# Sketched attention and a squared-ReLU FFN on one core: order of loads, casts, squares and GpSimd work

## The chip, the core and the metric

The kernel runs on one core of a Trainium2 chip. The core has a matrix engine (TensorE, PE in the profile), three engines for elementwise work (VectorE or DVE, ScalarE or ACT, GpSimd or POOL), and DMA engines that move data between memory (HBM) and the on-chip memories. A DMA is issued from an engine's instruction stream: here from SyncE (SP), which does nothing else, and from ScalarE. Each engine works through its own instructions in the order in which the program gives them, and waits where an instruction needs something that another engine has not yet finished. The metric is the device time of one execution in microseconds (us), told as the median of several runs.

## The reference

The input is q, k and v for 4 batches, 4 heads, 1088 tokens and 32 columns a head, two small sketches S1 and S2 (8 x 32), and two weights w_in (128 x 2048) and w_out (2048 x 128). All are 32-bit floats.

```
phi(x) = outer product of (S1 x) and (S2 x), 64 features a token
kv  = sum over tokens of phi(k) v          (64 x 32 a head)
z   = sum over tokens of phi(k)            (64 a head)
x   = phi(q) kv / (phi(q) z + 1e-6)        (heads side by side: 128 columns)
out = relu(x w_in)^2 w_out                 (4 * 1088 = 4352 tokens)
```

## The kernel before

The FFN is nearly all of the matrix work. Each batch of 1088 tokens is cut into column chunks of 384, 384 and 320 tokens, and the 2048 hidden features into 16 blocks of 128. One FFN step is one chunk with one block: 4 x 3 x 16 = 192 steps. In a step, `ffn1` (L677) multiplies the block of w_in, which is held as 16-bit floats, with the chunk of x into the PSUM tile `pg` (two buffers), a relu goes from `pg` to the SBUF tile `gt` (three buffers; on ScalarE at L691 or on VectorE at L693), and a square goes from `gt` to `g2` (on ScalarE at L697, or on VectorE or GpSimd at L699). `ffn2` (L703) multiplies the block of w_out with `g2`, in 32-bit floats, and adds it up in the PSUM tile `po` over the 16 blocks. `ffn2` of a step stands three steps behind `ffn1` of the same step in TensorE's order (LA = 3). So TensorE's order is: ffn1 of step i + 3, ffn2 of step i, then whatever attention work is placed in slot i. When a chunk is finished, VectorE scales and transposes `po` (`f_oT` and `f_ob` L767 for the first two chunks, `f_sc` and `f_sT` after), and SP writes it out.

The attention of the first chunk has to come before the first FFN step and forms the prologue (L826 to L926). In short: `s_nat` (L143) receives S1 and S2, is transposed into `s_T`, and is spread into several small layouts; k is transposed on VectorE (`a_kT`), multiplied with the sketch (`a_kf`), and its features are formed (`a_fs`, `a_kp`); `a_kv` (L306) and `a_z` add up kv and z; `a_kvz` transposes them (`kvt`) and spreads them (`kvz`); q is transposed (`a_qT`), multiplied with the sketch (`rep`, L847) and its products are formed; `a_nd` gives numerator and denominator; `a_x1`, `a_x2` (L604) and `a_x3` (L628) on VectorE divide, and scale each row by a factor so that it fits 16-bit floats (the output is multiplied by the factor's square, `beta`, later; `f_br` L735 spreads beta to 16 x 3 columns with 16 small GpSimd copies); `a_xp` and `a_xT` turn x. `keep_warm` (L826) gives TensorE matmuls on zeros while it has nothing else to do.

The loads of batch 0 (L143 to L177) stand in this order: ScalarE issues S1, S2 and later the last part of v; SP issues k in two pieces, q columns 0 to 383, v in eight pieces, q columns 384 to 1087, w_in in two halves, w_out in two halves. Eight completion semaphores are shared in turn by all these DMAs, so a DMA's issue also waits for the landing of the one eight before it. w_in is cast to 16 bits by two ScalarE copies of 1024 columns (L903).

The attention of all other chunks is put into the FFN steps. A small planner, `_Plan` (L24), keeps for each engine the time that is already placed in each step. `add` puts a task into the first step that is at least a fixed lag behind the tasks it needs and in which the engine's placed time with this task stays under a limit (0.95 us for TensorE, 1.2 and later 0.99 for VectorE, 0.6 for ScalarE, 5.0 for GpSimd). Tasks are added in the order in which they need each other: `old_chunk` (the second chunk of batch 0, in the prologue's style), then per chunk `feature_tasks` (the q products: `a_qg` on TensorE, shuffles `sh` on VectorE, multiplies `qpn` on GpSimd), `nd_tasks` (`a_ndn`), `x_tasks` (the division: `dT`, `de`, `rd`, `rb`, `x` on VectorE, `ax` on ScalarE, `sm` on TensorE, `rs` and `s` (`a_s2`) on VectorE, `xs` and `bt` on GpSimd; `xs` writes the tile `xT` that ffn1 of the next chunk reads), and per batch `k_tasks` and `kv_tasks` (`kp` half on VectorE, half on GpSimd; the sums `ks` on GpSimd; `a_kv9` on TensorE). Several of them use the same two PSUM buffers in turn (the planner's keys "N" and "X"): `a_kv9` of batch 1 can start only when `s` of the last chunk of batch 0 has read its buffer.

After that, `balance` (L1067) goes through the steps in order and chooses for each one which engine does its relu and which its square, by the estimated lateness of each engine. Then the main loop writes the program: for each step ffn1 with its relu and square, ffn2, and the tasks of that slot, in this order on every engine:

```
for i in range(NS + 4):
    if i + LA < NS:
        ffn1(i + LA, where[i + LA])
    if 0 < i < NS - NFF:
        ffn2(i)
    ...
    for f, args in P.slots[i]:
        f(*args)
```

The last chunk is handled apart: its steps form the output of one tile with tokens as rows, so that the end is short (`ffn2_tile`).

## Time and profile before

| what | value |
|---|---|
| time, median of 11 runs | 196.01 us (195.56 to 198.5) |
| the profiled execution's own time | 195.47 us |
| its span, first to last instruction | 193.6 us |
| mean TensorE clock granted | 0.996 of full |
| ffn2 matmuls (L709) | 143.8 us busy, mean 458 ns |
| ffn1 matmuls (L681) | 61.1 us busy, mean 317 ns |
| relu on ScalarE (L691) / VectorE (L693) | 124 of 457 ns / 69 of 533 ns |
| square on ScalarE (L697) / GpSimd (L699) | 159 of 506 ns / 31 of 774 ns |
| HBM traffic | 8.78 MB read, 2.23 MB written |

The profile comes from one execution. In its lines a place in the code is given as L and the line number of the listing above; an operation is written as output, arrow, input, with tile names. Busy times of TensorE add up to more than its share since matmuls overlap in the engine's pipeline: what counts there is the distance between the starts of successive matmuls. The timeline lists instructions as start, duration, engine, line, operation, shape and count (x2 means two alike were merged into one line); a bracket at the end tells how long the engine stood idle before and what released it. The chain of waits follows the end of the program back, at each instruction, to what released it. The table of stretches gives for each stretch of time its length, then busy time and instruction count for TensorE, its weight loads, VectorE, ScalarE and GpSimd, then the clock, the share of time at which the DMA engines were busy, and GB/s.

### The profile page before, as it was taken

To read this page: it belongs to the slowest core of one execution; us is meant where nothing else is said; L and a number is where in the kernel's file an instruction comes from. 1 tells how busy PE (TensorE), PEld (TensorE's weight loads), DVE (VectorE), ACT (ScalarE), POOL (GpSimd) and SP (SyncE) were. 2 spreads that over 40 slices of the span, in tenths; PEclk is the share of its full clock that TensorE was granted. 3 is DMA by queue.
4 is the path that set the end of the run, shared out by engine and by line. 5 is a ranking of instruction groups with operands and counts; after the bars stand their busy time and mean duration, and the time that the engine had idled before them with its cause. 6 is when DMAs were issued, how large, how long until landed. Compare 5 with 4: busy or idle time off the path is not lost.

```text
span 193.6 us, 4446 instructions
## 1 busy us (share of the span) xinstructions
PE 185.4 (96%) x1639; PEld 112.5 (58%) x1639; DVE 131.5 (68%) x326; ACT 141.2 (73%) x322; POOL 97.5 (50%) x162
## 2 busy tenths in 40 slices
PE   7997999989999999999999999999999999999990
PEld 2873755555666555565566555565566555556990
DVE  2966886985787559954876659864776555667740
ACT  3454996976787969866897969867787868767740
POOL 3844546990393838941473557951483932600000
PEclk9999999999999999999999999999999999999998
DMA  6799410020037320020057410020020110110201
GB/s 188 201 317 280 117 51 2 3 41 3 0 59 207 124 34 3 2 44 0 2 98 182 123 22 3 5 39 0 0 44 2 19 20 0 20 20 0 41 3 34
DMA packets 27199, 11.40 MB, mean 59 GB/s; under 512 B 19178, under 2 KB 25770, under 8 KB 27178
## 3 DMA queue, kind: packets, MB, share of 16 engines
q1 hardware_dynamic: 26726, 11.02, 23.2%
q8 instruction: 13, 0.21, 0.5%
q10 hardware_dynamic: 452, 0.10, 0.2%
q14 instruction: 8, 0.07, 0.1%
HBM read 8.78 MB, written 2.23 MB: 57 GB/s over the span
## 4 chain that ended last, share of the span: by engine, by line
PE 86%; DVE 7%; DMA 1%; ACT 1%; issue 1%; POOL 0%; ACTq 0%; DVEq 0%; POOLq 0%
PE po L709 54%; PE pg L681 15%; PE ndn L448 4%; PE kvp L314 3%; PE pt L726 2%; DMA s_nat<-in_S_dram 1%; PE qg L417 1%; PE rep L847 1%; PE kf L258 1%; DVE sh L426 1%; PE kvp L328 1%; PE kf L357 1%; PE kvp L576 1%; DVE ob L770 1%; PE sm L498 1%; PE nd L576 1%
## 5 line engine op out<-in xcount | busy, mean ns | idle before, releaser
L709 PE MATMUL po<-g,w_o 128*128 128x384 f32 (+3 forms) x386 | 143.8, 458 | 0.0
L697 ACT ACTIVATE g<-gt 128x384 f32<-128x384 f32 (+1 forms) x159 | 79.9, 506 | 21.3 <-DVE gt L693 17.6
L709 PEld LDWEIGHTS po<-g,w_o 128*128 128x128 f32 x386 | 66.1, 190 | 32.6 <-issue 22.5
L691 ACT ACTIVATE gt<-pg 128x384 f32<-128x384 f32 (+2 forms) x124 | 56.2, 457 | 13.8 <-PE pg L681 13.0
L681 PE MATMUL pg<-xT,w_in 128*128 128x384 f16 (+2 forms) x193 | 61.1, 317 | 0.7 <-ACT xT L660 0.3
L693 DVE TENSOR_SCALAR gt<-pg 128x384 f32<-128x384 f32 (+1 forms) x69 | 36.7, 533 | 26.5 <-PE pg L681 25.4
L699 POOL TENSOR_TENSOR g<-gt 128x384 f32<-128x384 f32 (+1 forms) x31 | 23.8, 774 | 47.1 <-ACT gt L691 46.8
L681 PEld LDWEIGHTS <-w_in 128*128 128x128 f16 x193 | 18.8, 98 | 24.0 <-issue 6.6
L435 POOL TENSOR_TENSOR qp<-sh 128x384 f32<-128x384 f32 (+1 forms) x20 | 19.1, 961 | 6.9 <-DVE sh L426 5.1
L426 DVE STREAM_SHUFFLE sh<-qg 128x384 f32<-128x384 f32 (+1 forms) x40 | 21.4, 562 | 0.0
L458 DVE STREAM_TRANSPOSE dT<-ndn 128x384 f32<-128x384 f32 (+1 forms) x10 | 5.4, 543 | 11.3 <-PE ndn L448 11.3
L284 POOL TENSOR_TENSOR kp<-fs 128x1152 f32<-128x1152 f32 x3 | 9.5, 3167 | 5.3 <-DVE fs L277 5.3
L522 POOL TENSOR_TENSOR xT<-x,rs 128x384 f16<-128x384 f32 (+1 forms) x10 | 9.5, 947 | 1.7 <-DVE rs L513 1.7
L741 POOL COPY br<-beta 32x3 f32<-32x3 f32 x32 | 6.5, 204 | 5.6 <-DVE beta L642 4.3
L448 PE MATMUL ndn<-qp,kw 64*32 64x192 f32 (+1 forms) x320 | 8.4, 318 | 0.0
L531 POOL TENSOR_TENSOR bt<-s 128x384 f32<-128x384 f32 (+1 forms) x10 | 7.8, 781 | 0.9 <-DVE s L504 0.9
L448 PEld LDWEIGHTS ndn<-qp,kw 64*32 64x32 f32 x320 | 4.7, 106 | 5.2 <-issue 3.8
L340 POOL TENSOR_TENSOR ks<-kp 128x1024 f32<-128x1024 f32 x3 | 7.1, 2366 | 0.2
L513 DVE TENSOR_SCALAR rs<-sm 128x384 uint32<-128x384 uint32 (+1 forms) x10 | 5.2, 522 | 2.5 <-PE sm L498 2.5
L314 PE MATMUL kvp<-kp,vn 128*32 128x64 f32 (+1 forms) x288 | 5.9, 221 | 0.7 <-DVE s L504 0.7
L351 POOL TENSOR_TENSOR ks<-ks 128x512 f32<-128x512 f32 (+1 forms) x6 | 6.2, 1032 | 0.5
L314 PEld LDWEIGHTS kvp<-kp,vn 128*32 128x32 f32 (+1 forms) x288 | 4.7, 109 | 2.8 <-DVE s L504 1.3
(119 smaller groups left out, 157.3 us busy)
## 6 DMA issues: line engine op xcount, KB each, us to landing
vn<-in_v_dram SPq DMA_DIRECT2D x32, 64.0 KB, 4.0
kn<-in_k_dram SPq DMA_DIRECT2D x3, 544.0 KB, 11.2
qn<-in_q_dram SPq DMA_DIRECT2D x3, 544.0 KB, 3.6
out_dram<-oT SPq DMA_DIRECT2D x24, 48.0 KB, 1.9
w_in<-in_moe_w_in_dram SPq DMA_DIRECT2D x2, 512.0 KB, 4.7
w_o<-in_moe_w_out_dram SPq DMA_DIRECT2D x2, 512.0 KB, 9.5
out_dram<-oT SPq DMA_DIRECT2D x12, 40.0 KB, 1.7
out_dram<-ob SPq DMA_DIRECT2D x8, 48.0 KB, 1.8
```

What stands on the lines that cost most here:

```text
L284: (nc.vector if g == 0 else nc.gpsimd).tensor_tensor(out=_ap(st[b, "kp2"], 0, 128, 128 * NT * g, [[64, 2 * NT], [8, 8], [1, 8]]), in0=_ap( ...
L314: nc.tensor.matmul(st[b, "kvp"][32 * h : 32 * h + 32, 0:64], _ap(vn[b], 0, n, v0 + dv * h, [[1, 32]]), kp[0:n, at[h] : at[h] + 64], start= ...
L426: nc.vector.stream_shuffle(in_=_ap(st[b, "qg", ch], 0, 128, 0, [[512, 2], [1, n]]), out=_ap(t_, 0, 128, 0, [[n, 2], [1, n]]), mask=mask_q[ ...
L435: nc.gpsimd.tensor_tensor(out=qp[:, 0 : 2 * n], in0=st[b, "sh", ch, s, 0][:, 0 : 2 * n], in1=st[b, "sh", ch, s, 1][:, 0 : 2 * n], op=mult,)
L448: nc.tensor.matmul(nd[32 * h : 32 * h + 32, 512 * g + 192 * i : 512 * g + 192 * i + n], st[b, "kw"][64 * g : 64 * g + 64, 128 * i + 32 * h ...
L522: nc.gpsimd.tensor_tensor(out=st[b, "xT"][:, 384 * ch : 384 * ch + n], in0=st[b, "x", ch][:, 0:n], in1=st[b, "rs", ch][:, 0:n], op=mult,)
L681: nc.tensor.matmul(pg[:, c0:c1], w_in[:, 128 * c : 128 * c + 128], st[b, "xT"][:, 384 * ch + c0 : 384 * ch + c1],)
L691: nc.scalar.activation(gt[:, c0:c1], pg[:, c0:c1], Relu)
L693: nc.vector.tensor_scalar(out=gt[:, c0:c1], in0=pg[:, c0:c1], scalar1=0.0, scalar2=None, op0=amax)
L697: nc.scalar.activation(g2[:, c0:c1], gt[:, c0:c1], Square)
L699: (nc.vector if on[1] == "DVE" else nc.gpsimd).tensor_tensor(out=g2[:, c0:c1], in0=gt[:, c0:c1], in1=gt[:, c0:c1], op=mult)
L709: nc.tensor.matmul(st["po", b, ch][:, c0:c1], w_o[:, 128 * c : 128 * c + 128], g2s[i][1][:, c0:c1], start=first, stop=(c == NFF - 1), skip ...
```

## The change

Loads: S2 is issued by SP as its second DMA (ScalarE keeps S1); q columns 384 to 1087 are loaded in two pieces; SP's order behind v becomes w_in first half, q 384 to 767, w_out first half, q 768 to 1087, w_in second half, w_out second half. The unused rows of the last tile of v are set to zero, and the kv sum of that tile runs over 128 rows instead of 64.

Prologue: the transpose of q columns 384 to 767 moves from behind the numerators to before `kvt`; that of the other columns moves to the end of the prologue. ScalarE casts only the first half of w_in; the second half becomes two casts of 512 columns on GpSimd, the first two tasks of GpSimd in the FFN steps. `a_qg` for the third chunk moves from the prologue to behind the ffn1 of step 2, and `f_br` of the first chunk into the FFN steps. `a_x2` gets by with four VectorE operations instead of five: the scale is a power of two taken from the float's exponent bits, and beta is formed from the same bits behind `xs` by two operations instead of one.

FFN steps: a square on ScalarE is no longer written directly behind its relu, but kept in a list (`due`) and written behind the relu of the next step; in the last chunk it stays where it was. The planner gives GpSimd tasks intervals of time (length divided by 0.85) instead of a limit per step, with the finish of the interval counted for what follows; some assumed durations change (kp 2.7 to 3.15, ks2 2.0 to 2.3, br 2.4 to 3.6); `balance` takes the length of a step and of its relu and square from the columns, and gives GpSimd no square in a step whose successor has a GpSimd task. The tasks' slots and the engines for relu and square are worked out anew from this.

```
@@ _Plan @@
-        self.late = []
+        self.pool = []
...
+        if eng == "POOL":
+            d, t = dur / 0.85, float(s)
+            for t0, t1 in sorted(self.pool):
+                if t + d <= t0:
+                    break
+                t = max(t, t1)
+            self.pool.append((t, t + d))
+            s = int(t)
+            self.fix(key, eng, dur, s, f, *args)
+            self.at[key] = max(s, int(t + d - 0.6))
+            return s
@@ loads of batch 0 @@
-    def load_qk(dst, src, b, c0, c1):
-        nc.sync.dma_start(
+    def load_qk(dst, src, b, c0, c1, eng=nc.sync):
+        eng.dma_start(
...
-    for s_, r0 in ((S1, 0), (S2, 8)):
-        nc.scalar.dma_start(s_nat[r0 : r0 + 8, :], s_[:, :])
+    nc.scalar.dma_start(s_nat[0:8, :], S1[:, :])
...
-    nc.scalar.copy(zero_a[:, :], zero[:, 0:8])
     alloc_loads(0)
     load_qk(kn[0], k, 0, 0, 512)
+    nc.sync.dma_start(s_nat[8:16, :], S2[:, :])
     load_qk(kn[0], k, 0, 512, S)
     load_qk(qn[0], q, 0, 0, 384)
     load_v(vn[0], 0, 0)
     load_v(vn[0], 0, 2, (nc.scalar, nc.scalar))
+    nc.scalar.copy(zero_a[:, :], zero[:, 0:8])
     load_v(vn[0], 0, 1)
-    load_qk(qn[0], q, 0, 384, S)
     w_in32 = cpool.tile([128, DFF], F32)
     w_in = cpool.tile([128, DFF], F16)
     w_o = cpool.tile([128, DFF], F32)
-    for c in range(2):
-        nc.sync.dma_start(
+    def load_w_in(c, eng):
+        eng.dma_start(
             w_in32[:, 1024 * c : 1024 * c + 1024], moe_w_in[:, 1024 * c : 1024 * c + 1024]
         )
-    for c in range(2):
+    def load_w_o(c):
         nc.sync.dma_start(
             _ap(w_o, 0, 128, 1024 * c, [[128, 8], [1, 128]]),
             bass.AP(
...
             ),
         )
+    def w_cast(c0, n, copy):
+        copy(w_in[:, c0 : c0 + n], w_in32[:, c0 : c0 + n])
+    load_w_in(0, nc.sync)
+    load_qk(qn[0], q, 0, 384, 768)
+    load_w_o(0)
+    load_qk(qn[0], q, 0, 768, S)
+    load_w_in(1, nc.sync)
+    load_w_o(1)
...
+    nc.gpsimd.memset(vn[0][64:128, 1024:1152], 0.0)
@@ a_kv @@
-        n = 64 if b == 0 and t == 8 else 128
+        n = 128
@@ a_x2, a_x3 @@
-        mm, mp, rm = (small(x, 1) for x in ("mm", "mp", "rm"))
-        nc.vector.tensor_tensor(out=m1[:, :], in0=mx[:, :], in1=rden[:, :], op=mult)
+        mm, rm = (small(x, 1) for x in ("mm", "rm"))
+        nc.vector.scalar_tensor_tensor(
+            out=m1[:, :], in0=mx[:, :], scalar=1e-20, in1=rden[:, :], op0=amax, op1=mult
+        )
         nc.vector.tensor_reduce(
             out=mm[:, :], in_=_ap(m1, 0, 128, 0, [[4, 3], [1, 4]]),
             axis=AX, op=amax, apply_absolute_value=True,
         )
         nc.vector.tensor_scalar(
-            out=mp[:, :], in0=mm[:, :], scalar1=1.0 / 1024.0, scalar2=1.0 / 1024.0,
-            op0=mult, op1=add,
-        )
-        nc.vector.reciprocal(rm[:, :], mp[:, :])
-        nc.vector.tensor_tensor(
+            out=rm[:, :].bitcast(U32), in0=mm[:, :].bitcast(U32),
+            scalar1=EXP, scalar2=EXP, op0=band, op1=bxor,
+        )
+        nc.vector.scalar_tensor_tensor(
             out=_ap(sc, 0, 128, 0, [[4, 3], [1, 4]]),
-            in0=_ap(rden, 0, 128, 0, [[4, 3], [1, 4]]),
+            in0=_ap(rden, 0, 128, 0, [[4, 3], [1, 4]]), scalar=512.0,
             in1=_ap(rm, 0, 128, 0, [[1, 3], [0, 4]]),
-            op=mult,
-        )
-        st[b, "x2", ch] = sc, mp
+            op0=mult, op1=mult,
+        )
+        st[b, "x2", ch] = sc, mm
...
         if o + n == 3:
-            nc.vector.tensor_tensor(
-                out=st[b, "beta"][:, 3 * ch : 3 * ch + 3], in0=mp[:, :], in1=mp[:, :], op=mult,
+            mp = wpool.tile([128, 3], F32, tag="mp", name="mp")
+            nc.vector.tensor_scalar(
+                out=mp[:, :].bitcast(U32), in0=mm[:, :].bitcast(U32),
+                scalar1=EXP, scalar2=None, op0=band,
+            )
+            nc.vector.scalar_tensor_tensor(
+                out=st[b, "beta"][:, 3 * ch : 3 * ch + 3], in0=mp[:, :], scalar=2.0**-20,
+                in1=mp[:, :], op0=mult, op1=mult,
             )
@@ ffn1 @@
+    due = []
+    def square_due():
+        while due:
+            dst, src = due.pop()
+            nc.scalar.activation(dst, src, Square)
...
+        square_due()
         if on[1] == "ACT":
-            nc.scalar.activation(g2[:, c0:c1], gt[:, c0:c1], Square)
+            due.append((g2[:, c0:c1], gt[:, c0:c1]))
+            if i >= NS - NFF:
+                square_due()
         else:
             (nc.vector if on[1] == "DVE" else nc.gpsimd).tensor_tensor(
@@ prologue @@
         a_z(0, *st[0, "kp", t], t == 8)
     nc.scalar.copy(qb[:, 0:128], rep[2, 0][:, 0:128])
     products(0, 128)
+    a_qT(0, 384, 768)
...
     a_kvs(0)
-    for c in range(2):
-        nc.scalar.copy(
-            w_in[:, 1024 * c : 1024 * c + 1024], w_in32[:, 1024 * c : 1024 * c + 1024]
-        )
+    w_cast(0, 1024, nc.scalar.copy)
     for t in range(3):
         a_nd(0, t)
-    a_qT(0, 384, S)
     a_qc(0, 1, psf, "po")
-    a_qg(0, 2)
...
     a_qb(0, 1)
-
-
-    f_br(0, 0)
+    a_qT(0, 768, S)
     P = _Plan(NS + 4, {"PE": 0.95, "DVE": 1.2, "ACT": 0.6, "POOL": 5.0, "SP": 9.0})
@@ tasks, planner, balance @@
-        P.add(("br", b, ch), "POOL", 2.4, [("x3", b, ch)], f_br, b, ch)
...
-            P.add(("kp", n, g), ("DVE", "POOL")[g], (1.36, 2.7)[g], [("fs", n, g)], a_kp2, n, g)
+            P.add(("kp", n, g), ("DVE", "POOL")[g], (1.36, 3.15)[g], [("fs", n, g)], a_kp2, n, g)
...
-        P.add(("ks2", n), "POOL", 2.0, [("ks1", n)], a_ks2, n)
+        P.add(("ks2", n), "POOL", 2.3, [("ks1", n)], a_ks2, n)
...
+    for i in range(2):
+        P.fix(("w", i), "POOL", 0.65, i, w_cast, 1024 + 512 * i, 512, nc.gpsimd.tensor_copy)
+        P.pool.append((float(i), i + 0.7))
     feature_tasks(0, 2)
+    P.add(("br", 0, 0), "POOL", 3.5, [], f_br, 0, 0)
...
+        if n == 1:
+            P.add(("br", 0, 1), "POOL", 3.6, [("x3", 0, 1)], f_br, 0, 1)
...
-            w = 0.8 if steps[s_][1] < 2 else 0.667
-            cost = {"ACT": 0.48 * w / 0.8, "DVE": 0.56 * w / 0.8, "POOL": 0.95 * w / 0.8}
-            time = w + load["PE"][s_]
+            n1, n2 = (min(384, S - 384 * steps[i_][1]) for i_ in (s_ + LA, s_))
+            cost = {"ACT": (n1 + 30) / 960, "DVE": (n1 + 140) / 960, "POOL": (n1 + 20) / 440}
+            time = n1 / 2400 + n2 / 600 + load["PE"][s_]
...
-                if q_ == "POOL" and (late[q_] + own_[q_] > 1.0 or end_ >= -1):
+                if q_ == "POOL" and (late[q_] + own_[q_] > 1.0 or load["POOL"][s_ + 1] > 0 or end_ >= -1):
@@ main loop @@
         ffn1(i, ("ACT", ("DVE", "ACT")[i % 2]))
+    a_qg(0, 2)
     for cols in ((0, 128), (128, 384)):
         ffn2(0, cols)
...
         if i + LA < NS:
             ffn1(i + LA, where[i + LA])
+        else:
+            square_due()
```

More of the change, by code (lines that the diff above doesn't have):

```diff
@@ L633, in a_x3 @@
             st[b, "xs", ch] = wpool.tile([128, 3 * 128], F16, tag="xs", name="xs")
-        sc, mp = st[b, "x2", ch]
+        sc, mm = st[b, "x2", ch]
         nc.vector.tensor_tensor(
@@ L823, in last_tile, with keep_warm @@
         store(b, 6, ob, 128, nc.sync)
-    def keep_warm(n, cols=512):
+    def keep_warm(n):
         t_ = st["warm"]
         for _ in range(n):
-            nc.tensor.matmul(t_[:, 0:cols], zero[:, 0:128], zero[:, 0:cols])
+            nc.tensor.matmul(t_[:, 0:512], zero[:, 0:128], zero[:, :])
     st["warm"] = psf.tile([128, 512], F32, tag="pg", name="warm")
```

## The prediction

> **What bounds the kernel now.** I read the page first: busy time and the chain that ended last.
>
> ```profile
> PE 185.4 (96%) x1639; PEld 112.5 (58%) x1639; DVE 131.5 (68%) x326; ACT 141.2 (73%) x322; POOL 97.5 (50%) x162
> PE 86%; DVE 7%; DMA 1%; ACT 1%; issue 1%; POOL 0%; ACTq 0%; DVEq 0%; POOLq 0%
> ```
>
> TensorE carries 86% of the chain. From 19.65 us on, the timeline of TensorE shows one FFN step each 0.81 us for 384 columns (0.67 for 320), which is the length of its own matmuls. Those are not touched, so a gain can come only from the stretch before the first FFN matmul (16.93 us) and from places where TensorE leaves this spacing. The chain of waits up to 20 us gives the first (start, length, work):
>
> ```profile
> 1.55 2.80 DMA s_nat<-in_S_dram
> ...
> 4.48 0.21 DVE s_T L229
> ...
> 11.00 1.49 PE rep L847 x6
> 12.49 1.51 PE kvp L576 x12
> ...
> 15.38 0.18 DVE mp L615
> 15.59 0.19 DVE rm L619
> ```
>
> S1 and S2 set the first 4.4 us; DVE's small operations carry it from 14.1 to 16.0. The timeline of TensorE gives the second:
>
> ```profile
> 38.63 0.81 PE L709 MATMUL po<-g,w_o 128*128 128x384 f32 x2
> 39.40 0.32 PE L681 MATMUL pg<-xT,w_in 128*128 128x384 f16 x1
> 40.33 0.32 PE L681 MATMUL pg<-xT,w_in 128*128 128x384 f16 x1
> 40.49 0.81 PE L709 MATMUL po<-g,w_o 128*128 128x384 f32 x2
> 42.01 1.21 PE L314 MATMUL kvp<-kp,vn 128*32 128x64 f32 x72 [0.71 <-DVE s L504]
> ```
>
> The ffn1 matmuls stand 0.93 apart instead of 0.81 (two steps, 0.26 lost), and the kv matmuls come at 42.01 where 40.49 + 0.65 + 0.1 = 41.24 was possible (0.77 lost). That is 1.03 us, the only such place before 178 us; near 179 us another 0.3 is lost in the last chunk, whose order the change leaves alone. Why 0.93? ScalarE's timeline:
>
> ```profile
> 33.76 0.47 ACT L691 ACTIVATE gt<-pg 128x384 f32<-128x384 f32 x1
> 34.26 0.53 ACT L697 ACTIVATE g<-gt 128x384 f32<-128x384 f32 x1
> 34.69 0.47 ACT L691 ACTIVATE gt<-pg 128x384 f32<-128x384 f32 x1
> ...
> 64.54 0.85 ACT L691 ACTIVATE gt<-pg 128x384 f32<-128x384 f32 x2
> ```
>
> Relu to its own square takes 0.50 from start to start, square to the next relu 0.43: 0.93 a pair, TensorE's spacing at 39 us. Where two relus follow one another (64.54: two of 0.47 in 0.85) the second starts 0.85 - 0.47 = 0.38 after the first. Waiting for the relu's result thus costs about 0.13 per pair.
>
> **The change part by part, on the profiled execution** (195.47 us, span 193.6; the median of the runs, 196.01, lies 0.54 above it, and I add the sum to the median).
>
> *S2 on SP's queue, second.* Before, ScalarE issues S1 at 0.93 and S2 at 1.55, which lands some 2.8 us later. On SP it is issued at about 1.2, behind the first k load, which landed at 3.47 (0.75 + 2.7). s_T then waits for DVE's first transpose (3.50 + 0.71 = 4.21) and not for 4.48: -0.3; bounds 0 and -0.34. SP's later DMAs move: from the third v load on, each waits for an older DMA's landing (8.8 us of issue for what takes 0.47 each), so little of S2's 0.47 is left at w_in; I count 0.2.
>
> *q columns 384 to 767 transposed before kvt.* DVE idles 0.99 us there (10.07 to 11.07), and the transpose takes 0.53 (as qT at 5.92), so it is free if the data is there. But this DMA now stands behind 512 KB of w_in.
>
> ```profile
> 6.63 0.43 SPq L110 DMA_DIRECT2D qn<-in_q_dram  x1
> 7.11 0.90 SPq L166 DMA_DIRECT2D w_in<-in_moe_w_in_dram  x2
> ...
> ```
> ```profile
> 7.70:11.00 3.30, 3.30 (x150) 2.78 (x149) 1.95 (x4) 0.55 (x3) 2.92 (x12) 1.00 0.96 266
> 11.00:12.40 1.40, 1.40 (x8) 1.02 (x7) 0.98 (x3) 0.73 (x3) 1.16 (x6) 1.00 1.00 393
> ```
>
> v's packets end at about 7.7; 512 + 192 KB (0.72 MB) at 266 GB/s (last column) take 2.7 us, at 393 GB/s 1.8. With 0.2 for S2 and 0.35 to land (as the difference between packets and landing of the first k load) the q columns arrive between 10.1 and 11.0. DVE is ready at 9.8, kvz is needed by 11.8 (rep's products start then), so arrival up to 10.45 is free and each later tenth costs a tenth: 0 to +0.8, I take +0.3, near the slower window, which has the same w_in half in it. Queued behind the waiting transpose are kvt, kvz and the products, and for them the nd matmuls.
>
> *x2 in four operations instead of five.* One of 0.2 from start to start falls out of the chain (15.38 to 15.59): -0.2. The extra operation for beta stands behind xs, beside the transposes on TensorE: 0.
>
> *Second half of w_in cast on POOL, 2 x 512 columns.* ScalarE loses a cast of 1.05 that ended at 14.2, idle until 16.6: 0. POOL's price: its CAST of 128 columns takes 0.29; its MEMSETs of 128 and 384 columns (0.21, 0.42) rise 0.85 ns a column, its multiplies 1.7, so 0.6 to 0.9 each. They are needed at FFN step 8, after 23 us; that cover is 6 us. What they can hurt is DVE. The lines:
>
> ```profile
> 32.39 3.12 POOL L284 TENSOR_TENSOR kp<-fs 128x1152 f32<-128x1152 f32 x1 [1.22 <-DVE fs L277]
> ...
> 34.40 1.14 DVE L467 TENSOR_SCALAR de<-dT 128x10 f32<-128x10 f32 x1
> ```
>
> A TENSOR_SCALAR on ten columns (0.17 elsewhere) lasted until POOL's multiply ended at 35.51. w_in's second half is now behind 0.36 MB of q, 0.5 MB of w_in and 0.5 MB of w_o, the same bytes that ended before at about 14.0; landed at 14.2 to 14.8, the casts run somewhere in 14.2 to 16.3, over x2 (14.98 to 16.0). Bounds: 0, and +1.2 if a small operation waits out each cast. Nearest in kind, a copy with one input, are POOL's copies of beta at 19.3 to 20.1: the DVE square beside them took 0.56, its usual time, and it was POOL that waited. So I take +0.2 and keep +1.2 for the range.
>
> [...]
>
> *qg of chunk 2 moved from TensorE's idle time (14.74) to behind ffn1 of step 2.* 16 matmuls, 0.50, and 0.1 for each change between kinds (the steps around ndn show it). In that place TensorE still loses 0.3 to 0.4 to relu (18.17, then 19.17 for 18.97), so of 0.7 I count +0.3; bounds 0 and +0.7. Its q columns arrive before 14, transposed on DVE behind qb (0.47, beside relu).
>
> *Squares a step behind.* A pair costs 0.37 + 0.43 = 0.80 in place of 0.93, TensorE's own 0.81. The 0.26 goes. The 0.77 goes too: kv9 is put five steps later, and the second half of its sum (POOL, 2.27 at 38.03) no longer stands beside ob, which took 1.62 instead of 0.56 there; s is then ready one us sooner. -1.0, bounds -0.3 and -1.1. What is late next: a square now ends about 0.8 later, and ffn2 reads it three steps after ffn1 began. For 384 columns: ready 0.43, relu, square and relu in turn 1.17, square 0.52, sum 2.1 of 2.6. For 320: 0.38 + 1.0 + 0.47 = 1.85 of 2.13, and an ax between (0.5) overruns it by 0.2. Three such chunks, of which the planner gives the first no relief on DVE: +0.2, bounds 0 and +0.9.
>
> *The rest: 0.* br (16 copies, 3.5) moves into POOL's idle time, needed at 34; if POOL were late, ob and its DMAs alone would wait. The interval bookkeeping puts xs as near as four steps (2.7 us) before its chunk; rs 0.55, xs 1.0 and waits make 2.0, so 0.7 of cover. vn's memset runs at 1.4, long before use.
>
> Sum: -0.3 + 0.3 - 0.2 + 0.2 + 0.3 - 1.0 + 0.2 = -0.5: 196.0 - 0.5 = 195.5 us.
>
> **The rivals.** (a) *The casts block x2*: +1.2 instead of +0.2, sum +0.5, 196.5, slower. For: the 1.14 row and the arrival estimate. Against: the copies at 19.3. It decides from a cast cost of 1.1 on. (b) *q waits behind w_in*: +0.8, sum 0, 196.0, no change. For: 0.96 DMA share at 7.7 to 11. Against: 393 GB/s right after. (c) *Squares late*: +0.9, sum +0.2, 196.2. For: 0.28 of slack only; against: DVE and POOL take relus and squares in most such steps. (d) *xs late at a chunk's start*: 0.7 of cover used up, 0.4 at four chunks: +1.1 on the sum, 196.9. For: four steps instead of nine and more; against: POOL is half idle. (e) *The start gains all it can*: q and casts free, qg in the idle 0.3: 194.8.
>
> **How the numbers follow.** 0.2% is 0.39 us, about what a measurement of this kernel can tell from no change. Chances: forecast 0.45 (its own range 194.9 to 195.8; 0.42 faster, 0.03 same), (a) 0.22 (0.15 slower, 0.07 same), (b) 0.10 (0.08 same, 0.02 slower), (c) 0.07 (0.03 same, 0.04 slower), (d) 0.08 slower, (e) 0.08 faster. Faster 0.50, same 0.21, slower 0.29. The range goes from 194.5, (e) with the best kv place, to 197.0, which holds (a) to (d) one at a time.
>
> **What the profile after would show.** s_T at 4.2; the transpose of 384 q columns between 9.8 and 11.5, and kvt no later than 11.1; x2's operations 0.17 each, or one of 0.5 and more beside a POOL cast; xs at 15.8; ScalarE's relu and square 0.37 and 0.43 apart; no ffn1 spacing over 0.81 from 36 to 46 us; no wait before kvp. The prediction is wrong if xs starts after 16.2, if a new spacing over 0.7 shows in 320-column chunks, or if ffn1 waits at a chunk's start.

## The result and the profile after

The changed kernel takes 198.26 us (median of 12 runs, 196.47 to 200.22) against 196.01 before: the ratio is 1.0095, with an interval of 1.0079 to 1.0111. (Ratios here and below leave out a kernel's slow runs, those more than 1.5% above its fastest: of the changed kernel the three at 199.82 to 200.22 us, so that nine runs with a median of 197.86 are compared.) It is slower, and outside the predicted range of 194.5 to 197.0. The profile taken with the result is of an execution of 200.03 us, one of the three longest; a second trace of the same kernel (197.61 us, span 195.5; run 12 below) lies near the median, and the account below is made on it.

The page of the first trace: busy time, granted clock in 40 slices, chain.

```profile
PE 188.0 (95%) x1639; PEld 114.3 (58%) x1639; DVE 121.8 (62%) x312; ACT 138.6 (70%) x340; POOL 95.8 (48%) x161
...
PEclk9996699999999999999999999999999999999997
...
PE 87%; DMA 5%; DVE 3%; ACT 1%; SPq 1%; issue 1%; ACTq 0%; DVEq 0%
```

Two things are new: DMA has 5% of the chain instead of 1%, and in slices 4 and 5 (14.8 to 24.7 us) the clock of TensorE is at 0.6, where before every slice but the last was at 0.9 or more. The chain of waits of the second trace says which DMA:

```profile
7.23 5.14 DMA qn<-in_q_dram
12.37 0.02 issue
12.39 0.58 DVE qT L274
12.97 0.21 DVE kvt L395
...
13.85 2.01 PE kvp L598 x12
...
16.84 0.49 DVE m L632
...
17.76 0.51 DVE sc L643
```

The q columns 384 to 767 are issued at 7.23, are there 5.14 us later, and kvt, the numerators (kvp, 12 matmuls) and all that follows stand behind their transpose. The kernel before has kvt at 11.07 and the numerators at 12.37, and the two operations called m and sc take 0.17 each. VectorE, then TensorE:

```profile
11.07 0.32 DVE L373 STREAM_TRANSPOSE kvt<-kvp 128x128 f32<-128x128 f32 x1 [0.99 <-PE kvp L328]
...
14.98 0.17 DVE L610 TENSOR_TENSOR m<-mx,rden 128x12 f32<-128x12 f32 x1
...
15.80 0.17 DVE L620 TENSOR_TENSOR sc<-rden,rm 128x12 f32<-128x12 f32 x1
```

```profile
12.37 1.62 PE L576 MATMUL kvp<-kvz,qp 128*128 128x132 f32 x12
```

For the changed kernel (second trace) the timeline of VectorE gives the length of that wait in its bracket, and next to it the two operations of a_x2 that have become long, m and sc:

```profile
12.39 0.58 DVE L274 STREAM_TRANSPOSE qT<-qn 128x384 f32<-128x384 f32 x1 [2.65 <-DMA qn<-in_q_dram]
12.89 0.27 DVE L395 STREAM_TRANSPOSE kvt<-kvp 128x128 f32<-128x128 f32 x1
...
15.96 0.17 DVE L616 TENSOR_SCALAR den<-kvp 128x12 f32<-128x12 f32 x1 [1.59 <-PE kvp L598]
...
16.84 0.48 DVE L632 SCALAR_TENSOR_TENSOR m<-mx,rden 128x12 f32<-128x12 f32 x1
17.36 0.17 DVE L635 TENSOR_REDUCE mm<-m 128x3 f32<-128x12 f32 x1
17.55 0.17 DVE L639 TENSOR_SCALAR rm<-mm 128x3 uint32<-128x3 uint32 x1
17.76 0.50 DVE L643 SCALAR_TENSOR_TENSOR sc<-rden,rm 128x12 f32<-128x12 f32 x1
```

GpSimd's timeline shows a cast beside each of those two. Of the two short ones between them, mm ran beside no cast, and rm had begun 0.07 before the second cast:

```profile
16.69 0.61 POOL L192 CAST w_in<-w_in 128x512 f16<-128x512 f32 x1 [4.70 <-DMA w_in<-in_moe_w_in_dram]
17.36 0.20 POOL L974 MEMSET vn<- 64x128 f32 x1
17.62 0.61 POOL L192 CAST w_in<-w_in 128x512 f16<-128x512 f32 x1
```

m ends at 17.32, the first cast at 17.30; sc ends at 18.26, the second cast at 18.23. The table of stretches (stretch, length, five engines' busy time, clock, DMA share, GB/s) shows the third loss:

```profile
12.00:14.00 2.00, 0.15 (x1) 0.18 (x2) 1.50 (x5) 0.80 (x2) 0.00 (x0) 1.00 1.10 367
14.00:15.00 1.00, 1.00 (x10) 1.00 (x11) 0.37 (x2) 0.52 (x1) 0.00 (x0) 0.94 1.03 337
15.00:18.00 3.00, 3.00 (x9) 1.42 (x8) 1.87 (x7) 0.00 (x0) 1.19 (x3) 0.50 1.10 338
18.00:19.00 1.00, 0.67 (x3) 0.13 (x3) 0.96 (x4) 0.09 (x1) 0.23 (x1) 0.85 1.14 204
```

TensorE is busy for 0.15 of the 2 us before 14.0, and once it works again its clock is 0.50 from 14.9 to 18.3. In the first trace there are two such stretches, 14.6 to 18.0 and 21.4 to 24.8.

What the prediction hoped for in the FFN steps did come, but for one spacing. TensorE's timeline around kv9 in the first trace, then ScalarE's:

```profile
48.45 0.33 PE L717 MATMUL pg<-xT,w_in 128*128 128x384 f16 x1
48.61 0.81 PE L748 MATMUL po<-g,w_o 128*128 128x384 f32 x2
49.26 0.33 PE L717 MATMUL pg<-xT,w_in 128*128 128x384 f16 x1
49.42 0.81 PE L748 MATMUL po<-g,w_o 128*128 128x384 f32 x2
50.16 1.21 PE L336 MATMUL kvp<-kp,vn 128*32 128x64 f32 x72
```

```profile
43.10 0.51 ACT L711 ACTIVATE g<-gt 128x384 f32<-128x384 f32 x1
43.51 0.47 ACT L727 ACTIVATE gt<-pg 128x384 f32<-128x384 f32 x1
43.88 0.52 ACT L711 ACTIVATE g<-gt 128x384 f32<-128x384 f32 x1
44.29 0.48 ACT L727 ACTIVATE gt<-pg 128x384 f32<-128x384 f32 x1
```

From 44.41 on the ffn1 matmuls stand 0.81 apart up to kvp (the two spacings around an sm matmul at 43.33 are still 0.94 and 0.95), and kvp follows 0.74 after the last ffn2 pair begins, with no bracket; relu to square takes 0.37, square to relu 0.41.

Step by step, the second trace against before, by the starts of the same matmuls: numerators 1.48 later (13.85 for 12.37); their length 2.00 for 1.62, 0.38 more, at half clock; from den to xs 2.33 for 1.90, 0.43 more; so the first ffn1 comes 2.29 later (19.22 for 16.93). From the ffn1 of step 2 to that of step 7, where qg now stands, 0.29 more. (Steps are numbered from 0, as in the kernel; the expectations below count the two parts of step 0's ffn1 singly, so that their steps 3 and 8 are 2 and 7 here.) From there to the last ffn1, 0.65 less. Sum 1.93; the spans differ by 1.9.

### The profile page after: what moved, and what is told of

It is laid out like the page before. It is cut to its first block, busy times and chain, and to the rows that moved or that the text cites. A ratio compares the mean times of both kernels' runs of the same rounds, so it can differ in the third digit from the quotient of the medians.

```text
span 197.9 us, 4533 instructions
## 1 busy us (share of the span) xinstructions
PE 188.0 (95%) x1639; PEld 114.3 (58%) x1639; DVE 121.8 (62%) x312; ACT 138.6 (70%) x340; POOL 95.8 (48%) x161
## 4 chain that ended last, share of the span: by engine, by line
PE 87%; DMA 5%; DVE 3%; ACT 1%; SPq 1%; issue 1%; ACTq 0%; DVEq 0%
PE po L748 57%; PE pg L717 16%; PE ndn L470 4%; DMA qn<-in_q_dram 2%; DMA vn<-in_v_dram 2%; PE qg L439 2%; PE pt L765 2%; PE kvp L336 2%; PE kvp L598 1%; PE sm L520 1%; PE kf L379 1%; PE nd L598 1%; SPq L131 1%; ACT gt L727 1%; ACT g L711 1%
## 5 line engine op out<-in xcount | busy, mean ns | idle before, releaser
L727 ACT ACTIVATE gt<-pg 128x384 f32<-128x384 f32 (+2 forms) x139 | 65.6, 474 | 30.0 <-PE pg L717 29.1
L729 DVE TENSOR_SCALAR gt<-pg 128x320 f32<-128x320 f32 (+1 forms) x54 | 28.3, 524 | 33.7 <-PE pg L717 26.8
L738 POOL TENSOR_TENSOR g<-gt 128x384 f32<-128x384 f32 (+1 forms) x27 | 21.6, 805 | 48.7 <-ACT gt L727 48.7
L448 DVE STREAM_SHUFFLE sh<-qg 128x384 f32<-128x384 f32 (+1 forms) x40 | 20.4, 561 | 0.0
L274 DVE STREAM_TRANSPOSE qT<-qn 128x384 f32<-128x384 f32 (+1 forms) x12 | 6.3, 542 | 2.8 <-DMA qn<-in_q_dram 2.7
L780 POOL COPY br<-beta 32x3 f32<-32x3 f32 x32 | 5.9, 183 | 1.2
L299 DVE STREAM_TRANSPOSE fs<-kf 128x288 f32<-128x288 f32 x6 | 2.5, 462 | 6.2 <-PE kf L379 6.2
```

What stands on the lines that cost most here:

```text
L448: nc.vector.stream_shuffle(in_=_ap(st[b, "qg", ch], 0, 128, 0, [[512, 2], [1, n]]), out=_ap(t_, 0, 128, 0, [[n, 2], [1, n]]), mask=mask_q[ ...
L727: nc.scalar.activation(gt[:, c0:c1], pg[:, c0:c1], Relu)
L729: nc.vector.tensor_scalar(out=gt[:, c0:c1], in0=pg[:, c0:c1], scalar1=0.0, scalar2=None, op0=amax)
L738: (nc.vector if on[1] == "DVE" else nc.gpsimd).tensor_tensor(out=g2[:, c0:c1], in0=gt[:, c0:c1], in1=gt[:, c0:c1], op=mult)
```

## Experiments

Each is timed against the kernel before on the same chip (its medians were 195.7 to 196.0 us); a ratio is to that. "Mean clock" is the granted clock over one run.

**1. The transpose of q columns 384 to 767 put back.**

```
     products(0, 128)
-    a_qT(0, 384, 768)
...
         a_nd(0, t)
+    a_qT(0, 384, 768)
```

> The changed kernel, with one instruction put back: the transpose of q columns 384 to 767 stands behind the numerators again, not before kvt. Theory W (the wait for these columns is the loss): in the changed kernel's trace VectorE stands still for 2.74 us before this transpose, kvt starts at 13.21, and TensorE is idle from 12.1 to 14.17; then the granted clock falls to 0.5 for some 3.5 us and the numerators take 2.6 us instead of 1.6. Without the wait kvt starts at 10.6 to 10.9, TensorE's hole closes, the clock stays at 1.0, and the step-6 ffn1 comes about 5 us earlier than 25.34: 194.3 to 195.2 us, under the kernel before. Theory L (the lateness is made in the FFN steps: the qg behind ffn1 of step 2 and the later squares): the first ffn1 comes earlier, but the time stays at 196.3 or more.

Measured: 195.30 us (10 runs), ratio 0.998 (0.9954 to 1.0007). In the trace the transpose starts at 13.46 without waiting, kvt at 11.65, the first ffn1 at 17.30, and the clock stays at 1.0. One instruction's place on VectorE takes the ratio from 1.0095 to 0.998, some 2.3 us. That is not the wait alone: m and sc take 0.17 here, since a_x2 is over before the first cast starts (17.73, when its half of w_in has landed), so the casts' price goes with it. Theory W holds; the time came out just above the upper edge of what was expected (195.2), since kvt was later than I said (more on that under the hardware) and since step 2 to step 7 kept the 0.30 of qg. From step 7 to the last ffn1 this trace gains 0.66.

**2. TensorE's hole filled, the wait left.**

```
+    st["warm"] = psf.tile([128, 512], F32, tag="pg", name="warm")
+    keep_warm(9)
     a_kvs(0)
```

> The changed kernel, with nine matmuls on zeros (512 columns, 16-bit, about 0.21 us each by the prologue's own) put into TensorE's hole from 12.1 to 14.2 us. The wait for the q columns stays. Theory W with a clock that falls because of the hole: kvt still at 13.0 to 13.3, but the clock stays at 1.0 up to 18 us, the numerators take 1.6 us, the steps 3 to 5 lose no more than before, and the step-6 ffn1 comes at 22.6 to 23.6 instead of 25.34: 196.0 to 197.0 us. Rival (the clock falls for something else, such as the small holes between 18.7 and 21.4): 0.5 is still seen at 22 to 24 us and the time stays within 0.5 of the changed kernel's 197.9.

Measured: 199.32 us (4 runs: three with a mean clock of 0.979 to 0.986 at 199.3 to 200.1, one with 0.995 at 196.90). The first half of the expectation holds: kvt late again at 13.57, no half clock up to 20.2, the 12 numerators in 1.51. The time does not (196.0 to 197.0 was expected), and neither does the rival's: m (0.62) and sc (0.50) are held up by the casts, xp comes after a hole that has grown to 1.63, and the half clock comes from 20.3 to 23.7 instead. In this trace, filling one hole moved the stretch to after the next one. The fourth run had no such stretch, by its mean clock, and its 196.9 is the price of wait and casts by themselves, from one run only.

**3. GpSimd's casts after its copies of beta.**

```
+    f_br(0, 0)
     for i in range(2):
         P.fix(("w", i), "POOL", 0.65, i, w_cast, ...)
-    P.add(("br", 0, 0), "POOL", 3.5, [], f_br, 0, 0)
+    P.add(("br", 0, 0), "POOL", 3.5, [], lambda *a: None, 0, 0)
```

> The changed kernel, with the 16 copies of beta ahead of the two GpSimd casts of w_in, so that the casts no longer run beside a_x2 (17.60 to 18.21 and 18.54 to 19.15 us in its trace). Theory P (the casts hold VectorE up): the two operations that took 0.45 and 0.50 (m and sc) take 0.17 to 0.2 as m and sc did before, xs starts 0.6 earlier against den, and the time falls by 0.4 to 0.7 us from the changed kernel's 197.9. Rival (the new form with two operations and a scalar takes that long by itself on 12 columns): both still take 0.45 to 0.50, and nothing changes beyond 0.2.

Measured: 197.12 us, ratio 1.0057 (1.0025 to 1.009). Its VectorE timeline:

```profile
18.22 0.17 DVE L632 SCALAR_TENSOR_TENSOR m<-mx,rden 128x12 f32<-128x12 f32 x1
...
18.83 0.17 DVE L643 SCALAR_TENSOR_TENSOR sc<-rden,rm 128x12 f32<-128x12 f32 x1
19.04 0.62 DVE L658 TENSOR_TENSOR xs<-kvp,sc 128x128 f16<-128x128 f32 x2
```

The same instructions take 0.17; den to xs is 1.70 (17.34 to 19.04) instead of 2.33. Theory P holds: the casts cost 0.63, and a_x2 with four operations is 0.20 shorter than with five (1.70 for 1.90).

**4. The q columns ahead of w_in.**

```
-    load_w_in(0, nc.sync)
     load_qk(qn[0], q, 0, 384, 768)
+    load_w_in(0, nc.sync)
     load_w_o(0)
```

> The changed kernel, with one pair of DMAs exchanged: q columns 384 to 767 are issued directly behind v, and the first half of w_in after them. Theory W: the columns land at 9.2 to 10.0 instead of 12.67, VectorE's transpose of them waits less than 0.3, kvt starts at 10.5 to 10.8, the clock stays at 1.0: 194.2 to 195.2 us. The first w_in half lands at about 12.5 to 13.3, still ahead of its cast's user at 16.5. Rival (not the order but the sharing of the DMA engines makes a transfer of 192 KB take 4.9 us, wherever it stands): landing after 11.5, the time above 196.5.

Measured: 195.70 us, ratio 1.0011 (0.9983 to 1.004). The landing is as theory W said:

```profile
9.46 0.49 DVE L892 TENSOR_TENSOR qp<-rep,qb 128x128 f32<-128x128 f32 x2
9.87 0.57 DVE L274 STREAM_TRANSPOSE qT<-qn 128x384 f32<-128x384 f32 x1
10.67 0.32 DVE L395 STREAM_TRANSPOSE kvt<-kvp 128x128 f32<-128x128 f32 x1 [0.24 <-PE kvp L350]
```

No bracket before the transpose. The time is above what I expected, and the runs fall into two groups: six with a mean clock of 0.993 to 0.995 take 195.07 to 195.72, four with 0.986 to 0.987 take 196.35 to 197.09. The trace belongs to the second: TensorE, then the table of stretches.

```profile
14.07 0.81 PE L869 MATMUL warm<-zero 128*128 128x512 f16 x3
15.74 0.62 PE L680 MATMUL xp<-iden,xs 128*128 128x128 f16 x3 [0.86 <-DVE xs L658]
```

```profile
16.00:18.60 2.60, 2.01 (x25) 1.00 (x26) 2.05 (x9) 2.27 (x7) 1.26 (x3) 1.00 1.10 311
18.60:22.00 3.40, 3.40 (x10) 1.93 (x9) 3.40 (x13) 1.77 (x5) 0.16 (x1) 0.52 0.64 135
```

So the moved qg has a second price: it had filled TensorE's time before xp, and that hole is now 0.86 instead of 0.36.

**5 to 8** went on from there. Run 5 puts qg back into the prologue (and loads q in one piece, so that its columns are there):

```
-    load_w_in(0, nc.sync)
-    load_qk(qn[0], q, 0, 384, 768)
-    load_w_o(0)
-    load_qk(qn[0], q, 0, 768, S)
+    load_qk(qn[0], q, 0, 384, S)
+    load_w_in(0, nc.sync)
+    load_w_o(0)
...
     a_qc(0, 1, psf, "po")
+    a_qT(0, 768, S)
+    a_qg(0, 2)
...
-    a_qT(0, 768, S)
...
-    a_qg(0, 2)
```

> The changed kernel, with two things as in the kernel before: q columns 384 to 1087 are loaded in one piece directly behind v, ahead of w_in, and qg of the third chunk (with the transpose of its q columns) stands in the prologue behind qc, not behind the ffn1 of step 2. The first 384 of these columns are still transposed before kvt, the w_in casts stay on GpSimd, S2 on SP, the squares a step behind. Reference for it is the run with q ahead of w_in (195.7 us; in its trace 1.03 us of hole before xp, then the clock at 0.5 from 18.9 to 22, and in its runs 195.1 to 195.7 where the mean clock was 0.993 to 0.995 and 196.4 to 197.1 where it was 0.986 to 0.987). Theory G (qg had filled the hole, and costs 0.3 where it was put): the hole before xp shrinks to 0.3 to 0.5, no stretch at 0.5 follows, step 8 comes no later against step 3 than in the kernel before (5.2 to 5.3 us instead of 5.5 and more): 194.6 to 195.1 us with all runs above 0.993. Rival (the drop is made by something else, qg is free): 195.3 to 195.9 us, and some runs still at 0.987.

Measured: 195.18 us, ratio 0.9969 (0.9941 to 0.9997). Neither theory is right as it stood. qg's own price is confirmed by the trace of run 7, which has the same start and no half clock: from step 2 to step 7 it takes 4.69 us (4.63 before), where runs 1, 8 and 12, with qg in between, take 4.93. (The lengths in my expectation were read off wrongly; the difference of 0.3 is what counts.) But 5 of 12 runs still have a mean clock of 0.987 to 0.988 (195.87 to 196.75; the others 194.20 to 195.25), though the bracket before xp is down to 0.33 in the trace, which belongs to these five. (The expectations give holes from the modelled end of the last matmul, 0.16 more than the brackets.) In one piece the q columns also land later: the transpose waits 0.53 for them, until 10.73.

Run 6 issues S2 from ScalarE again.

```
     nc.scalar.dma_start(s_nat[0:8, :], S1[:, :])
+    nc.scalar.dma_start(s_nat[8:16, :], S2[:, :])
...
-    nc.sync.dma_start(s_nat[8:16, :], S2[:, :])
```

> The kernel of the run before, and S2 issued by ScalarE again, behind S1. Theory D (S2 as SP's second DMA delays the second k load by more than it brings s_T forward): s_T back at 4.4 to 4.5 instead of 4.1, but the second k load lands at 4.2 to 4.5 instead of 4.5 to 5.7, the second kT transpose starts at 5.1 to 5.2 in place of 4.9 to 5.8, kvt is as early or earlier: the same time or up to 0.4 less than the run before, with a smaller spread. Rival (my prediction's step: S2 on SP is worth 0.3): 0.2 to 0.4 us slower than the run before.

Measured: 195.01 us, ratio 0.9947 (0.9926 to 0.9969): no difference to run 5 (0.9969) that these intervals can tell. The mechanism is as theory D has it: the second k load lands at 4.23, where with S2 ahead of it it landed between 4.51 and 5.74 in seven traces; s_T starts at 4.38 instead of 4.07 to 4.25, and the second transpose of k at 5.06 instead of 4.88 to 5.76. What the first transposition wins, the second loses.

Run 7 is run 5 with each square directly behind its relu.

```
             due.append((g2[:, c0:c1], gt[:, c0:c1]))
-            if i >= NS - NFF:
-                square_due()
+            square_due()
```

> The kernel of the first run of this group, with every ScalarE square written directly behind its own relu again; the engines chosen for relus and squares and all tasks' places stay. Theory Q (my prediction's step: squares a step behind take away the 0.13 us a pair that ScalarE waits for its relu): relu to square is again 0.50, the ffn1 spacing grows to 0.9 or more in several stretches of 384 columns, 0.3 to 1.0 us slower than the first run of this group. Rival (what was regained between steps 23 and 32 came from the later place of kv9 and the GpSimd intervals alone): within 0.2 of that run.

Measured: 197.89 us, ratio 1.0086 (1.0054 to 1.0117), 2.7 us more than run 5. TensorE's timeline has the old spacing of 0.93 back, and in more places than the kernel before:

```profile
40.59 0.32 PE L716 MATMUL pg<-xT,w_in 128*128 128x384 f16 x1
40.75 0.81 PE L746 MATMUL po<-g,w_o 128*128 128x384 f32 x2
41.52 0.32 PE L716 MATMUL pg<-xT,w_in 128*128 128x384 f16 x1
41.68 0.81 PE L746 MATMUL po<-g,w_o 128*128 128x384 f32 x2
42.45 0.32 PE L716 MATMUL pg<-xT,w_in 128*128 128x384 f16 x1
```

Theory Q holds, and more strongly than I had put it. The new choice of engines gives ScalarE 139 relus and 163 squares (124 and 159 before) and VectorE 54 relus (69 before): it counts on the shorter pair. Without the shorter pair the new plan is worse than the old one by 2.3 us (from step 7 to the last ffn1).

Run 8 is run 4 with more matmuls on zeros before xp.

```
-    WARM0, WARM = 10, 3
+    WARM0, WARM = 10, 6
```

> The run with q ahead of w_in, and six matmuls on zeros instead of three in the place before xp, where its trace shows 1.03 us without TensorE work. Theory H (the clock falls because of holes in TensorE's work of 0.8 us and more in the start): the hole is 0.4 or less, no stretch at 0.5 follows, all runs have a mean clock of 0.993 or more, and the time is 195.1 to 195.5 us with the high group (196.4 to 197.1) gone. Rival (the clock falls for other reasons): the two groups stay, median 195.6 to 196.

Measured: 195.21 us, ratio 0.9965 (0.9948 to 0.9982), and all 12 runs at a mean clock of 0.993 or more (194.70 to 195.60). Against 4 of 10 in run 4 the high group is gone, with nothing else changed. Theory H holds for this hole.

**9. All together:** run 5, S2 on ScalarE, and WARM = 5.

> Everything learned so far in one kernel: q columns 384 to 1087 in one piece ahead of w_in, qg of the third chunk in the prologue, S2 on ScalarE, and five matmuls on zeros instead of three before xp (0.43 us more, into a hole that the trace of the run with qg put back shows as 0.49). What is left of the change: the early transpose of 384 q columns, half of w_in's cast on GpSimd, the shorter a_x2, the squares a step behind and the planner. Theory (holes in the start lower the clock; each part's own worth adds up): all runs at a mean clock of 0.993 or more, 194.2 to 194.9 us, faster than both kernels. Rival (the hole is not the cause): runs at 0.987 to 0.988 remain, median 195.0 to 195.3.

Measured: 194.93 us, ratio 0.9941 (0.9912 to 0.9971). It beats both kernels; one of 12 runs is at 0.986, so the expectation that all would stay at 0.993 or more missed by one.

**10. The squares a step behind, alone, on the kernel before.**

```
         if on[1] == "ACT":
-            nc.scalar.activation(g2[:, c0:c1], gt[:, c0:c1], Square)
+            due.append((g2[:, c0:c1], gt[:, c0:c1]))
```

(with `square_due` and its calls as in the change.)

> The kernel before, and one part of the change alone: ScalarE's squares a step behind, with the engines and places that the old planner chose. My prediction's step, cut to this part: the two ffn1 spacings of 0.93 near 39 us become 0.81 (0.26 gained), the 0.77 of wait before kvp stays mostly, since s comes no earlier; squares that come late in chunks of 320 columns cost 0 to 0.3: 195.4 to 195.9 us against 195.8. Rival (the squares a step behind are worth as much here as in the new plan, where writing them behind their own relu again cost 2.7 us): 194.5 us or less.

Measured: 195.71 us, ratio 0.9977 (0.9953 to 1.0001). The time is as expected, the working only in part. The timeline of TensorE:

```profile
40.04 0.33 PE L688 MATMUL pg<-xT,w_in 128*128 128x384 f16 x1
40.21 0.81 PE L719 MATMUL po<-g,w_o 128*128 128x384 f32 x2
41.90 1.21 PE L314 MATMUL kvp<-kp,vn 128*32 128x64 f32 x72 [0.88 <-DVE s L504]
```

Of the two spacings of 0.93, the second is now 0.81, but the first, behind an sm matmul, stays at 0.95: 0.16 is gained ahead of kvp, not 0.26. And kvp waits 0.88 instead of 0.71: what the squares win, kv9's wait takes back, because s is no earlier. In the first chunk of 320 columns one ffn1 spacing is 0.83 where it was 0.67 (54.11 to 54.94), so that from step 7 to the last ffn1 this trace loses 0.17.

**11. The old start with the new FFN steps.** S2, the loads, the transposes, qg, both casts and the first copies of beta as before; the shorter a_x2, the zeroed rows of v and everything else from `_Plan` on as in the change.

> The changed kernel with the whole start as in the kernel before (S2 on ScalarE, q in one piece ahead of w_in, its transpose and qg behind the numerators, both casts of w_in on ScalarE, the first copies of beta in the prologue), but for the shorter a_x2; the FFN steps are those of the changed kernel (squares a step behind, GpSimd intervals, the later kv9, the new choice of engines). Theory (the FFN part is worth 0.67 as the traces without a slow stretch showed, a_x2 0.2): 194.8 to 195.2 us against 195.8. Rival (the FFN part gains only because GpSimd's casts and copies were moved with it): 195.5 us or more.

Measured: 194.58 us, ratio 0.9941 (0.9907 to 0.9976), a little better than expected. From step 7 to the last ffn1 its trace gains 0.60. Run 9, timed on the same chip, keeps the early transpose and the casts on GpSimd and is no faster (194.93): no run shows a gain from the new start beyond the shorter a_x2.

**12. The changed kernel again** (no edit).

> The changed kernel as it is, once more, for a second trace. Theory W: the q columns 384 to 767 land after 12 us again, kvt comes after 12.6, TensorE has a hole of 1.4 us or more before the numerators, and at least one stretch at a clock of 0.5 follows; a run with one such stretch is 1 to 2 us shorter than the first trace's 200.0, which had two. Rival (the late landing was a disturbance of that one execution): kvt before 11.5 and a time near 195.5.

Measured: 197.61 us with one stretch at half clock; this is the second trace above. Theory W holds: the columns are late in every trace of the changed load order (12.39, 12.71, 12.88 and 13.07 for the transpose that waits for them; in run 1, where none waits, their packets end at 12.13).

**13. The kernel of run 11 with four matmuls on zeros instead of three.**

> The kernel with the old start and the new FFN steps (194.58 us; 3 of its 12 runs at a mean clock of 0.986 to 0.987 and 196.3 to 197.4 us, the others at 194.0 to 195.6), and four matmuls on zeros before xp instead of three; its trace has 0.31 us of hole there, the fourth takes 0.21. Theory (small holes in the start let the clock fall in some runs): no run at 0.987, median 194.3 to 194.8. Rival (a hole of 0.3 does nothing, these runs have another cause): again 2 to 4 of 12 at 0.987, the others unchanged.

Measured: 194.95 us, ratio 0.9971 (0.9938 to 1.0005), 2 of 12 runs at 0.986. The rival holds: runs at lower clock are left with the hole filled, so a hole of 0.3 us does not explain them (2 of 12 and 3 of 12 are too few to tell apart).

## Why the prediction was wrong

The sum was -0.5; the second trace has +1.9. Term by term:

- *q columns (+0.3, bounds 0 and +0.8)*: the numerators came 1.48 later, and this is the step that failed. I had them arrive "between 10.1 and 11.0", from 0.72 MB that must pass after v's end at 7.7, at 266 to 393 GB/s. In the trace they were in use from 12.39. The packets of 1536 bytes, which at that time only this load has, run from 9.76 to 12.02. From 7.8 to 12.0 1.0 MB were moved, some 240 GB/s, and not 0.72: w_out's first half, issued 0.48 behind q, travelled beside it. So the transfer did not end when the bytes ahead of it and its own had passed, and both ends of my range rested on that. By these figures the 0.28 MB more made about 1.2 us of the lateness, and 240 instead of 266 GB/s for the 0.72 MB another 0.3 (an estimate). The 1.48 is a difference between two traces and holds S2's part and the scatter of the start: the three traces with this wait and no filler begin the numerators at 13.85 to 14.35, the ten in which nothing waits for q at 11.91 to 13.02. The rate that I took as the better bound (393) came from a stretch with other transfers.
- *What queues behind the wait*: I had listed kvt, kvz, the products and the numerators, and priced each tenth of lateness at a tenth. But an idle TensorE (0.15 us of work from 12.0 to 14.0) also lost its clock (0.50 from 14.9 to 18.3): 0.38 in this trace, and in the first trace, with two stretches, step 7 comes 5.05 late instead of 2.58. No term of the sum had it, though the page gave the clock a row of its own.
- *Casts on GpSimd (+0.2, bounds 0 and +1.2)*: measured 0.63 (run 3). The bound held it, the choice within it failed, and that the casts met a_x2 at all was not for the reason given: I had their data land at 14.2 to 14.8, over a_x2, but the first cast was released at 16.69, and it met a_x2 only because a_x2 was late too; in run 1 a_x2 is over before the casts start, and they cost it nothing. That the 0.63 lay within the bounds is in part luck. As "nearest in kind" I took copies that had begun after a VectorE square and had to wait themselves, and read from them that VectorE is not held up. The 1.14 us row, in which the GpSimd operation was first (32.39, the VectorE operation at 34.40, their ends at 35.51 and 35.54), was the nearer one. In the second trace m and sc, begun 0.15 and 0.14 after the casts, end within 0.03 us of them (17.32 and 17.30, 18.26 and 18.23); mm, the tensor_reduce beside no cast, takes 0.17, and so does rm, which began 0.07 before the second cast.
- *Four operations for five (-0.2)*: -0.20 (run 3). *qg behind ffn1 of step 2 (+0.3)*: +0.29 in the second trace, 0.30 in run 1. Both right. I had counted qg's old place as idle time that costs nothing to empty; runs 4 and 8 show that emptying it cost clock (4 of 10 runs at 0.986 to 0.987 with the hole of 0.86, none of 12 with it filled).
- *S2 (-0.3)*: nothing that the times can tell (run 6). I had priced what it was moved past at w_in only; it stands ahead of the second k load as well. (The 8.8 us of issue in the working belong to no row of the start: SP's eight v loads take 4.44 us there.)
- *Squares a step behind and kv9's place (-1.0)*: right in sum. -1.01 is what is left of the measured -0.65 when the 0.36 of the next term is taken out of it; the ffn1 spacing with kv9 in it, 3.05 before and 2.27 in the second trace, makes 0.78 of it. As put, 0.26 came from the squares and 0.77 from the place; runs 7 and 10 show that the two cannot be added up that way: squares alone lose 0.17 us from step 7 on, the plan alone loses 2.3, and together they gain 0.65.
- *Squares late (+0.2)*: 0.36, of it 0.25 in the place named. In the second trace, where sm follows an ax in a chunk of 320 columns:

```profile
59.07 0.33 PE L520 MATMUL sm<-ax,part 128*128 128x384 bf16 x1
59.24 0.30 PE L717 MATMUL pg<-xT,w_in 128*128 128x320 f16 x1
59.52 0.81 PE L748 MATMUL po<-g,w_o 128*128 128x320 f32 x2
60.16 0.30 PE L717 MATMUL pg<-xT,w_in 128*128 128x320 f16 x1
```

ffn1 to ffn2 is 0.28 here instead of 0.14, and the pair 0.81 instead of 0.70: 0.25. The other 0.11 is at the same kind of place in a chunk of 384 columns, where I had expected none: around the sm at 40.86 the ffn1 spacings are 0.94 and 0.95, and one of them would be 0.81.

With these: 1.48 + 0.38 - 0.20 + 0.63 + 0.29 - 1.01 + 0.36 = 1.93. Of the rivals, (a) and (b) were both right in kind and came together; I had weighed each alone, with the other at its small value, and so left out the case that both come with one cause: late data.

## What to carry to other kernels

Before an instruction is moved ahead of a chain, look at where its data stands in its DMA queue, and price the wait by when a load like it landed with as much queued behind it, not by bytes ahead over a bandwidth. Here the loads in one queue travelled beside one another, a later one too (in the second trace 1.0 MB were moved from 7.8 to 12.0 us, where the columns and what stood ahead of them are 0.72); the small load that something waits for goes first (run 4: one exchanged pair of lines, and the ratio is 1.0011 instead of 1.0095). Where TensorE set the time here, an idle hole early in the kernel was paid a second time through the clock (0.38 us of the numerators' length in the second trace), so cheap work that filled a hole was not free to move away (the high group of run 4, 1.4 us above its other runs on the mean). And a plan that counts on a change elsewhere (ScalarE's shorter pair) is to be tried with and without it before either is called good.

## What the runs showed of the hardware

**In these traces the clock falls in pieces of 3.41 us, and the pieces lie differently in each execution.** In all seven traces with half clock in the start each stretch lasts 3.41 us (after: 14.6 to 18.0 and 21.4 to 24.8; run 2: 20.3 to 23.7; run 4: 18.7 to 22.1), and in the 3.41 us before it TensorE was busy for 1.0 to 2.4 us. With TensorE as the bound a piece at half clock costs up to 1.7 us (an estimate, half of 3.41); the two groups of run 4 differ by 1.4 on the mean. The stretches of full clock are whole multiples of the same 3.413 us in all 15 traces, from 1 to 55 of them (before: one of 187.73 us, 55; the first trace: 10.24, 3.41 and 170.67 us, 3, 1 and 50), and the first on record begins at any time from 4.03 us (run 10) to 7.26 us (run 9). So in these traces the clock changed only at points 3.413 us apart, which lie differently in each execution, and one hole can fall into a single piece or be split between two.

That tells run 1 from run 4, whose traces have a hole of 0.87 and 0.86 us in the same place: in run 4 the piece from 15.32 to 18.73 has 2.37 us of TensorE work and half clock follows; in run 1 the pieces from 13.95 and from 17.36 have 2.44 and 2.89, and none follows. What decides is not settled: in run 3 a piece with 2.32 us (17.86 to 21.28) is followed by full clock. Nor does the length of a hole alone tell: holes of 2.0 us (second trace) and 0.86 us among smaller ones (run 4) were followed by half clock, and the one of 0.87 us in run 1 was not.

**The start scatters.** In the ten traces without a wait for q, kvt begins anywhere from 10.61 (run 11) to 11.72 (run 9), with the kernel before at 11.07. What makes it was not tried; it is as large as most parts of this change, so two single traces can't tell small parts of the start apart. Differences within one trace (a bracket, the time from den to xs, from step to step) are free of it; the 1.48 is not. Also open: why 2 to 5 of 12 runs of runs 5, 11 and 13 have a lower clock with holes no larger than those of the kernel before, of which 3 of 29 runs on one chip (197.22 to 197.85 us) are at 0.984 to 0.986 too. Run 6's longest execution, the one traced, shows a candidate: TensorE stands idle for 1.31 us before xp, put down to an operation that xp does not read, and half clock follows. No trace of run 11 or 13 with half clock was kept.
